# Order of a step's input loads, and the place of one gate tile, in a fused gated-linear-attention and FFN kernel

## The chip, the cores and the metric

The kernel runs on one core of a Trainium2 chip. The metric is device time of one execution in microseconds. A core has TensorE (PE in the profile, with its weight loads as PEld), VectorE (DVE), ScalarE (ACT), GpSimd (POOL), and SyncE (SP), which here issues nearly all DMAs from one queue in program order. Each engine runs its own instructions in order and waits on semaphores for the others.

## The reference

A recurrent attention over 32 heads-and-batches (batch 4, 8 heads, 768 positions, head size 48), and a feed-forward on its output with two multiplied gates and two further matrices:

```python
for t in range(S):
    state = alpha[:, :, t, :, None] * state + einsum('bhd,bhe->bhde', k[:, :, t], v[:, :, t])
    y[:, :, t] = einsum('bhd,bhde->bhe', q[:, :, t], state)
x = y.transpose(0, 2, 1, 3).reshape(B * S, H * D)        # 3072 x 384
out = ((x @ w1) * (x @ w2)) @ w3 @ w_out                 # d_ff 1024, out 3072 x 384
```

q, k, v and alpha come as float32, the four weights as float64.

## The kernel before, in words

**Tiling.** The sequence is cut into chunks of 128 positions, 6 to a batch, so N = 24 chunks over all. The loop of line 510 takes one chunk per step, n = 0 to 24. Three chunks make a group of 384 tokens, g = 0 to 7, on which the feed-forward gates work: one gate tile is `gate(g, f)`, 128 of the 1024 hidden columns for the 384 tokens of a group.

**Attention.** Within a chunk the decay is turned into sums of logarithms: `logs` (L246, ACT; from chunk 10 on also the casts L250 and L251) takes the logarithm of alpha, `decays` (L261 or L264) sums it on TensorE and takes two exponentials (L267, L268), and `decayed` (L277, DVE) multiplies k and q by them. `transposed` (L299, copied out at L301) turns k and q, `scores` (L339, masked at L342 on DVE) forms the products inside the chunk, `outer` (L311, added at L319 or L321) adds the chunk to the state, `attend_state` (L358) and `attend` (L364) form the output from the state and from the masked scores, and L368 copies it out. Every second chunk GpSimd rescales the state (`advance`, L328 to L330) by factors that go through DRAM (L253, L270, L272, L285). In one step these work on different chunks: `attend` on n - 1, `scores` and `outer` on n, `transposed` on n + 1, `decayed` on n + 2, `decays` on n + 3, `logs` on n + 4.

**Loads.** At the head of a step SP issues, in this order: the stores of x (L236) that the step before left, v of chunk n + 3 (L136, one of 5 buffers), alpha of chunk n + 5 (L124, 3 buffers), k and then q of chunk n + 4 (L130 and L131, 3 buffers). Later in the step come the weight loads (L181), the store of a finished gate tile (L419) and, in steps 4, 8, 12, 16 and 20, the load of a group's x back from DRAM (`load_x`, L379). A load waits until its buffer has been read; SP holds everything behind it meanwhile.

**Weights.** The float64 weights are taken apart as integers and put together as float32 on ACT and DVE (L189 to L199), a few instructions per step (`convert`). w1 and w2 are split into three parts each (L207, L209, L210), so that float32 products can be formed by fast matmuls.

**Gates.** Two steps after its load, in steps 6, 10, 14, 18 and 22, the x of a group is split in three (`split_x`: L385 on ACT, then L386 and L387 on DVE, each 128 by 1152). Half a gate tile is one call of `exact`: 6 matmuls of L396 into one PSUM bank, with the first and second part of the split, a scaled copy by ACT (L398), 3 matmuls of L400 into another bank, with the third part, and the sum on DVE (L401). Two halves are multiplied (L412) and stored (L419). The halves wait in a list, `fill`; `run(k)` puts k of them into the program at that point. From step 6 the number per step goes 0, 3, 3, 2, and starts again with every split: three places of a step take at most one half each.

```python
        pieces = (0, 3, 3, 2)[(n - 6) % 4] if n > 5 else 0
        ...
        run(pieces > 0)
        ...
        run(pieces > 1)
        ...
        run(pieces > 2)
```

Groups 0 to 3 put four of their eight tiles into the loop, group 4 (split in step 22, the last split of the loop) all eight into the list; steps 23 and 24 take three of these (six halves). Of the 64 tiles 45 are left for the time after the loop. There they run one after the other (line 572), with the conversion of w3 and w_out between them and, from some point on, a `fold` after a gate: w3 times w_out (L439, L441, L445 to L450), eight in all. When the last fold is done, buffers for the last stage are opened and the first four loads of stored gate tiles begin (L456). The last stage, `project`, splits these (L463 to L465) and multiplies them with the folded matrix (again L396 to L401), 24 times.

**Order of instructions.** The program text sets the order on PE and SP. On ACT and DVE the framework's scheduler orders the instructions by its own estimate of when their inputs come, so that a moved load can change their order too.

Of the kernel before, what the change touches and what calls it, by code (L numbers as in the profile page):

```python
# [48 lines left out]
def kernel(  # L49
# [27 lines left out]
    AHEAD = 4  # L77
# [39 lines left out]
    def rows(src, n):  # L117
        b, c = divmod(n, NCH)
        return src[b, :, ds(c * C, C), :].rearrange("h p d -> p h d")

    def load_a(n):
        if n < N:
            st["a", n] = inp.tile([C, H, D], FP32, tag="ac", name="ac")
            nc.sync.dma_start(out=st["a", n], in_=rows(alpha, n))  # L124

    def load_kq(n):
        if n >= N:
            return
        st["kq", n] = inp.tile([C, 2, H, D], FP32, tag="kq", name="kq")
        nc.sync.dma_start(out=st["kq", n][:, 0], in_=rows(k, n))  # L130
        nc.sync.dma_start(out=st["kq", n][:, 1], in_=rows(q, n))  # L131

    def load_v(n):
        if n < N:
            st["v", n] = vs[n % len(vs)]
            nc.sync.dma_start(out=st["v", n][:, :, 0:D], in_=rows(v, n))  # L136
# [77 lines left out]
    def convert(steps, ahead=3):  # L214

        for _ in range(steps):
            while weights and len(begun) < ahead:
                begun.append(weights.popleft())
                next(begun[-1])
            if not begun:  # L220
                return
            x = begun.popleft()
            try:
                next(x)
                begun.appendleft(x)
            except StopIteration:
                pass
# [4 lines left out]
    def store():  # L232

        while later:
            dst, src = later.popleft()
            nc.sync.dma_start(out=dst, in_=src)  # L236
# [4 lines left out]
    def logs(n):  # L241
        if n >= N:
            return
        a = st.pop(("a", n)).rearrange("p h d -> p (h d)")
        la = st["la", n] = work.tile([C, DM], FP32, tag="la", name="la")
        nc.scalar.activation(la, a, AF.Ln)  # L246
        if n >= LATE:

            t = st["la", n] = work.tile([C, 2, DM], FP32R, tag="la2", name="la2", bufs=1)
            nc.scalar.copy(t[:, 0], la)  # L250
            nc.vector.tensor_sub(t[:, 1], la, t[:, 0].bitcast(FP32))  # L251
        if n in ends:
            nc.gpsimd.dma_start(out=ends[n][2:3], in_=a[0:1])  # L253

    def decays(n):
        if n >= N:
            return
        lc = bank()[:, 0:DM]
        la = st.pop(("la", n))
        if n < LATE:  # L260
            nc.tensor.matmul(lc, utri if n % 2 else after, la, start=True, stop=True)  # L261
        else:
            for i in range(2):
                nc.tensor.matmul(lc, sums[:, n % 2], la[:, i], start=(i == 0), stop=(i == 1))  # L264

        e = st["e", n] = work.tile([C, 2, DM], FP32, tag="e", name="e", bufs=3)
        nc.scalar.activation(e[:, 0], lc, AF.Exp, scale=-1.0)  # L267
        nc.scalar.activation(e[:, 1], lc, AF.Exp)  # L268
        if n in ends:
            nc.gpsimd.dma_start(out=ends[n][0:1], in_=e[0:1, 0])  # L270
        if n + 1 in ends:
            nc.gpsimd.dma_start(out=ends[n + 1][1:2], in_=e[C - 1:C, 1])  # L272
        load_ends(n)
# [14 lines left out]
    def transposed(n):  # L288
        if n >= N:
            return  # L290
        qk = qks[n % 3]
        qkT = work.tile([C, 2, NP, C], FP32, tag="qkT", name="qkT")

        tp = [bank().rearrange("p (i j c) -> p i j c", i=2, j=NP) for _ in range(2)]
        for i in range(2):
            for j in range(NP):
                for half in range(2):
                    s = ds(DP * half, DP)
                    nc.tensor.transpose(tp[half][:, i, j, :], qk[s, i, 2 * j:2 * j + 2, :], ident[s, s])  # L299
        for half in range(2):  # L300
            nc.scalar.copy(qkT[:, :, :, ds(DP * half, DP)], tp[half])  # L301
        st["qkT", n] = qkT
# [20 lines left out]
    def advance(n):  # L323

        if n not in ends:
            return
        dec, d = work.tile([C, NP], FP32, tag="dec", name="dec"), decs[n // 2 % 2]
        nc.gpsimd.tensor_mul(dec, d[:, 0, :], d[:, 1, :])  # L328
        nc.gpsimd.tensor_mul(dec, dec, d[:, 2, :])
        nc.gpsimd.tensor_tensor(Ts[0][:, :, 0:D], st.pop(("T", n - 1)),  # L330
                                dec[:, :, None].to_broadcast([C, NP, D]), op=ALU.mult)

    def scores(n):
        qkT = st["qkT", n]
        sc = [bank().rearrange("p (j c) -> p j c", j=NP) for _ in range(2)]
        for j in range(NP):
            for i in range(2):
                r = ds(DP * i, D)
                nc.tensor.matmul(sc[i][:, j, :], qkT[r, 0, j, :], qkT[r, 1, j, :], start=True, stop=True)  # L339
        ms = work.tile([C, 2, NP, C], FP32, tag="ms", name="ms")  # L340
        for i in range(2):
            nc.vector.tensor_tensor(ms[:, i].bitcast(I32), sc[i].bitcast(I32), keep_bc, op=ALU.bitwise_and)  # L342
        st["ms", n] = ms
# [3 lines left out]
    def attend_state(n):  # L347
        qkT = st.pop(("qkT", n))

        y = [bank()[:, 0:HP * C].rearrange("p (j c) -> p j c", c=C) for _ in range(2)]
        st["y", n] = y, [(half * HP + j, i, y[i][ds(DP * half, DP), j, :])
                         for j in range(HP) for i in range(2) for half in range(2)]
        if n % NCH:
            for j, i, to in st["y", n][1]:
                r = ds(DP * i, D)
                nc.tensor.matmul(to, Ts[n % 2][r, j, :], qkT[r, 1, j, :],  # L358
                                 start=(j % HP == 0), stop=False, skip_group_check=True)
# [21 lines left out]
    def split_x(g, i):  # L381
        x = st.pop(("xT", g))
        t = tr[i].tile([C, 3, KM, TG], FP32R, tag="x3", name="x3")
        st["x3", g] = t
        nc.scalar.activation(t[:, 0], x, AF.Copy, scale=1.0 - 2.0 ** -13)  # L385
        nc.vector.tensor_sub(t[:, 1], x, t[:, 0].bitcast(FP32))  # L386
        nc.vector.scalar_tensor_tensor(t[:, 2], t[:, 0].bitcast(FP32), 1.0 + 1.0 / P, x,  # L387
                                       op0=ALU.mult, op1=ALU.subtract)
# [14 lines left out]
    def gate(g, f):  # L403
        r = []
        x = [[st["x3", g][:, part, kk, :] for kk in range(KM)] for part in range(3)]
        for i, scale in enumerate((1.0, P * P)):
            r.append(gw.tile([C, TG], FP32, tag="r", name="r"))
            exact(r[-1], [[w12[:, part, i, kk, ds(f * C, C)] for kk in range(KM)] for part in range(3)], x, scale)
            if len(r) == 1:
                yield  # L410
        ab = abp.tile([C, TG], FP32, tag="ab", name="ab")
        nc.vector.tensor_mul(ab, *r)  # L412
        store_ab()
        st["ab"] = g, f, ab
# [62 lines left out]
    def run(pieces):  # L477

        for _ in range(pieces):
            if not fill:  # L480
                return
            try:
                next(fill[0])
            except StopIteration:
                fill.popleft()
# [22 lines left out]
    begin = {4 + 4 * g: (g, range(FH if g < 4 else KF)) for g in range(5)}  # L508

    for n in range(N + 1):  # L510
        store()
        load_v(n + AHEAD - 1)
        load_a(n + 5)
        load_kq(n + AHEAD)
        if n:
            attend_state(n - 1)
        if n < N:
            scores(n)
        transposed(n + 1)
        if n - 2 in begin:  # L520
            g, tiles = begin[n - 2]
            split_x(g, 0)
            fill.extend(gate(g, f) for f in tiles)
        pieces = (0, 3, 3, 2)[(n - 6) % 4] if n > 5 else 0
        if n == 0:
            logs(2)
            decays(2)
            logs(3)
        early = n < 7
        convert(1, 2 if n == 0 else 3)  # L530
        advance(n)
        if n:
            attend(n - 1)
        outer(n)
        run(pieces > 0)
        if early:
            convert(1)
        decayed(n + 2)
        logs(n + 4)
        if n in begin:  # L540
            load_x(begin[n][0])
        convert(early and n > 2)
        run(pieces > 1)
        decays(n + 3)
        convert(early or n % 3 == 0)
        run(pieces > 2)
    store()
    part1.close()

# [79 lines left out]
```

## Time and profile before

| | us |
|---|---|
| median of 5 runs | 493.78 (491.25 to 495.92) |
| the profiled execution | 497.9 |
| its span, first to last instruction | 496.1 |
| mean granted TensorE clock in it | 0.976 of full |
| loop over chunks, to the last L364 | about 199 |
| PE of one gate tile at full clock (two times 1.04 and 0.52) | 3.12 |
| one projection on PE (2.77 and 1.39) | 4.16 |

The profile gives busy times per engine and, for the chain that ended last, what each piece waited for. A line of the chain has the start, the length and the work. A line of the timeline has the start, the length, the engine, the line of the kernel, the operation with its tiles and the count of instructions; in square brackets, where it applies, stands how long the engine was idle before it and what ended that idle time. The TensorE clock is either full (1.00) or half (0.50).

### The profile page before, as it was taken

How to read it: one execution, taken by the hardware profiler on the slowest of the kernel's cores; microseconds unless marked ns; L12 is line 12 of the kernel's file. 1: busy time of each engine (PE TensorE's matmuls, PEld its weight loads, DVE VectorE, ACT ScalarE, POOL GpSimd, SP SyncE). 2: the span in 40 equal slices, each digit the busy share in tenths (PEclk: the TensorE clock that was granted, in tenths of full speed). 3: DMA queues.
4: the chain of work that ended last, by engine and by line, in shares of the span. 5: the costliest groups of instructions: out<-in, count | busy, mean ns of one | idle time of the engine just before them, and what ended most of it. 6: DMA issues, size and time to landing. Idle time of an engine off the chain costs nothing.

```text
span 496.1 us, 9909 instructions
## 1 busy us (share of the span) xinstructions
PE 466.1 (94%) x3760; PEld 427.2 (86%) x3760; DVE 371.3 (75%) x620; ACT 250.1 (50%) x479; POOL 36.4 (7%) x83
## 2 busy tenths in 40 slices
PE   3788699999999998999999999999999999999997
PEld 1566489898998987999999988888888999999996
DVE  2779889997889575999999769686434787777771
ACT  2667667775667553555565345454223433333330
POOL 2132122121102200000000000000000000000000
PEclk9989989999799998999999999999999999999999
DMA  9999999899989963566555433320001886555511
GB/s 166 190 208 185 213 214 190 208 212 234 188 192 216 208 210 110 147 181 206 172 180 171 155 116 114 120 92 32 33 32 50 221 232 182 176 174 176 176 48 48
DMA packets 160496, 79.10 MB, mean 159 GB/s; under 512 B 104641, under 2 KB 154305, under 8 KB 160449
## 3 DMA queue, kind: packets, MB, share of 16 engines
q1 hardware_dynamic: 159168, 78.40, 62.4%
q0 software_dynamic: 1280, 0.08, 0.4%
q8 instruction: 29, 0.48, 0.4%
q14 instruction: 19, 0.15, 0.1%
HBM read 56.40 MB, written 22.06 MB: 158 GB/s over the span
## 4 chain that ended last, share of the span: by engine, by line
PE 84%; DMA 7%; ACT 3%; SPq 2%; DVE 2%; issue 1%; POOL 0%; ACTq 0%; POOLq 0%; DVEq 0%
PE bank L396 41%; PE bank L400 20%; PE bank L445 8%; PE bank L364 4%; PE bank L339 4%; DMA raw<-in_moe_w_dram 2%; PE bank L299 2%; PE bank L358 2%; PE bank L439 1%; DMA xd<-x 1%; DMA ac<-in_alpha_dram 1%; PE bank L311 1%; DMA dec<-ends 1%; PE bank L264 1%; DMA ends<-e 1%
## 5 line engine op out<-in xcount | busy, mean ns | idle before, releaser
L396 PE MATMUL bank<-x,w 128*128 128x384 f32 x768 | 161.4, 345 | 0.0
L396 PEld LDWEIGHTS bank<-x,w 128*128 128x128 f32 x768 | 136.4, 191 | 3.6 <-issue 0.5
L398 ACT ACTIVATE t<-bank 128x384 f32<-128x384 f32 x152 | 74.3, 491 | 116.7 <-PE bank L396 104.0
L401 DVE SCALAR_TENSOR_TENSOR r<-bank,t 128x384 f32<-128x384 f32 x128 | 69.7, 555 | 35.5 <-ACT t L398 29.4
L400 PE MATMUL bank<-x,w 128*128 128x384 f32 x384 | 87.5, 335 | 0.0
L396 PE MATMUL bank<-w3o,ab 128*128 128x384 f32 x384 | 70.4, 334 | 0.0
L400 PEld LDWEIGHTS bank<-x,w 128*128 128x128 f32 x384 | 69.0, 189 | 0.0
L396 PEld LDWEIGHTS bank<-w3o,ab 128*128 128x128 f32 x384 | 66.9, 188 | 0.0
L445 PE MATMUL bank<-wo,w3T 128*128 128x384 f32 x128 | 42.6, 486 | 0.0
L189 ACT ACTIVATE rest<-raw 128x512 f32<-128x512 uint32 (+1 forms) x36 | 23.4, 650 | 33.1 <-DMA raw<-in_moe_w_dram 25.8
L412 DVE TENSOR_TENSOR ab<-r 128x384 f32<-128x384 f32 x64 | 35.6, 557 | 2.2 <-DMA abd<-ab 1.4
L400 PE MATMUL bank<-w3o,ab 128*128 128x384 f32 x192 | 37.1, 334 | 0.0
L445 PEld LDWEIGHTS bank<-wo,w3T 128*128 128x128 f32 x128 | 24.2, 189 | 14.9
L464 DVE TENSOR_TENSOR ab<-abl,ab 128x1024 fp32r<-128x1024 f32 x24 | 29.4, 1225 | 9.1 <-ACT ab L463 9.1
L463 ACT ACTIVATE ab<-abl 128x1024 fp32r<-128x1024 f32 x24 | 25.5, 1062 | 19.0 <-PE bank L400 18.8
L339 PEld LDWEIGHTS bank<-qkT 48*128 48x128 f32 x384 | 25.0, 199 | 11.5 <-ACT qkT L301 5.6
L339 PE MATMUL bank<-qkT 48*128 48x128 f32 x384 | 29.8, 298 | 5.2 <-ACT qkT L301 3.0
L400 PEld LDWEIGHTS bank<-w3o,ab 128*128 128x128 f32 x192 | 33.6, 188 | 0.0
L342 DVE TENSOR_TENSOR ms<-bank,keep 128x512 int32<-128x512 int32 x48 | 31.2, 685 | 1.8 <-PE bank L339 1.8
L194 ACT ACTIVATE power<-power,rebias 128x512 uint32<-128x512 uint32 (+1 forms) x36 | 25.2, 702 | 11.5 <-DVE power L193 11.3
L277 DVE TENSOR_TENSOR qk<-kq,e 128x768 f32<-128x768 f32 x24 | 22.9, 954 | 9.7 <-ACT e L268 7.5
L401 DVE SCALAR_TENSOR_TENSOR o<-bank,t 128x384 f32<-128x384 f32 x24 | 13.4, 558 | 22.4 <-issue 13.7
(69 smaller groups left out, 544.7 us busy)
## 6 DMA issues: line engine op xcount, KB each, us to landing
abd<-ab SPq DMA_DIRECT2D x64, 192.0 KB, 2.6
abl<-abd SPq DMA_DIRECT2D x24, 512.0 KB, 4.5
raw<-in_moe_w_dram SPq DMA_DIRECT2D x16, 512.0 KB, 3.9
xT<-xd SPq DMA_DIRECT2D x12, 576.0 KB, 4.2
raw<-in_moe_w_dram SPq DMA_DIRECT2D x24, 256.0 KB, 4.9
ac<-in_alpha_dram SPq DMA_DIRECT2D x24, 192.0 KB, 5.0
kq<-in_k_dram SPq DMA_DIRECT2D x24, 192.0 KB, 5.2
kq<-in_q_dram SPq DMA_DIRECT2D x24, 192.0 KB, 4.3
```

The source lines that it names most:

```text
L189: nc.scalar.activation(rest, low, AF.Copy, scale=2.0 ** -52)
L194: nc.scalar.activation(power, power, AF.Relu, scale=2.0 ** 23, bias=rebias)
L339: nc.tensor.matmul(sc[i][:, j, :], qkT[r, 0, j, :], qkT[r, 1, j, :], start=True, stop=True)
L342: nc.vector.tensor_tensor(ms[:, i].bitcast(I32), sc[i].bitcast(I32), keep_bc, op=ALU.bitwise_and)
L396: nc.tensor.matmul(p1, w[part][i], x[part][i], start=(part == i == 0), stop=(part == 1 and i == n - 1))
L398: nc.scalar.activation(t, p1, AF.Copy, scale=(1.0 + 1.0 / P) * scale)
L400: nc.tensor.matmul(p2, w[2][i], x[2][i], start=(i == 0), stop=(i == n - 1))
L401: nc.vector.scalar_tensor_tensor(to, p2, -scale, t, op0=ALU.mult, op1=ALU.add)
L412: nc.vector.tensor_mul(ab, *r)
L445: nc.tensor.matmul(po, w3T[:, j, :], wo[:, j, :], start=(j == 0), stop=(j == KF - 1))
L463: nc.scalar.activation(t[:, 0], ab, AF.Copy, scale=1.0 - 2.0 ** -13)
L464: nc.vector.tensor_sub(t[:, 1], ab, t[:, 0].bitcast(FP32))
```

## The change

The four loads at the head of a step are issued with alpha first, then k and q, and v last. In the step of the last split, step 22, which takes no halves of gates today, the third place takes two: one whole gate tile of group 4. So one tile fewer is left after the loop, 44 instead of 45.

```diff
     for n in range(N + 1):
         store()
-        load_v(n + AHEAD - 1)
         load_a(n + 5)
         load_kq(n + AHEAD)
+        load_v(n + AHEAD - 1)
         if n:
             attend_state(n - 1)
...
         pieces = (0, 3, 3, 2)[(n - 6) % 4] if n > 5 else 0
+        final = n - 2 == max(begin)
...
         convert(early or n % 3 == 0)
-        run(pieces > 2)
+        run(2 if final else pieces > 2)
     store()
```

`begin` is the table of steps in which a group's x is loaded, so `max(begin)` is 20. In the list after the loop, the split of a further group is put in when four tiles are left before that group's first; with 44 tiles this falls on the first tile, with 45 on the second.

## The prediction

> **What bounds the kernel now.** I read the page's totals first, then the chain of work that ended last, then the timelines where that chain leaves TensorE.
>
> ```profile
> PE 466.1 (94%) x3760; PEld 427.2 (86%) x3760; DVE 371.3 (75%) x620; ACT 250.1 (50%) x479; POOL 36.4 (7%) x83
> ...
> PE 84%; DMA 7%; ACT 3%; SPq 2%; DVE 2%; issue 1%; POOL 0%; ACTq 0%; POOLq 0%; DVEq 0%
> ```
>
> The chain is 84% PE. In order of time it is PE without a break from 188.55 us to the end; the breaks that cost anything lie before. So a change pays only if PE stands less, or at less than full clock for less time, before 189 us. Up to about 64 us there are no gates, and the busy table in 5 us stretches shows DVE at 3.8 to 5.0 of 5 between 30 and 65: there the weight conversion on DVE sets the pace. From 70 to 121 PE is busy throughout but for 0.2 us near 92.
>
> **Part one: alpha, k, q, v instead of v, alpha, k, q.** No instruction is added; per step one v issue moves behind three others on SP. A v issue takes 0.41 us (at 50.15) to 1.05 us (at 18.46), so alpha, k and q leave that much earlier. v leaves later by three issues: around 50 us 0.90 + 2.51 + 2.17 = 5.6 us. It is for the outer product three steps later, and a step takes 7 to 9 us here; with that cover gone L311 would wait, and PE with it. The k issue waits for DVE (13 waits of L130, 22.2 us in all), and v used to slip in before that wait. Behind it now stand v and then the step's weight loads, ab store, xT load and the next x stores, each later by up to one v issue. I price that at 0 (bounds 0 and 1.05 us where one of them is late already), since the weight loads wait for DVE anyway (37.6 us at L181 in its three largest waits).
>
> Where is alpha late? Once on the chain:
>
> ```profile
> 50.60 6.87 DMA ac<-in_alpha_dram
> ...
> 57.50 0.52 ACT la L246
> 58.02 0.53 ACT w L207
> ...
> 58.58 0.42 DVE w L209
> ```
>
> ACT stood 0.53 us for it, so 0.53 is the most that this place can give. But L207 needs DVE's L199, which ended at 57.82, and it began at 57.93: with alpha in time it begins 0.1 us earlier. I take 0.1. q is late at 26.87 (DVE stood 1.68 us), but DVE's next work waits for weights that land at 29.56 and are not moved: 0.
>
> The compiled order also changes on ACT and DVE; on PE it does not until step 22. Three moves matter. (1) Near 32 us a 0.42 us L190 goes ahead of the L321 that waits 1.22 us for POOL: 0.3 gained. (2) Near 52 us the decayed qk (L277) goes ahead of L209, which could start at 51.72, and waits for an exponential I place at about 52.05 (L267 and L268 after a PE result near 50.6): 0.35 lost. (3) At the first gates:
>
> ```profile
> 66.88 0.49 ACT L398 ACTIVATE t<-bank 128x384 f32<-128x384 f32 x1 [2.64 <-PE bank L396]
> 67.27 0.64 ACT L368 COPY x<-bank 128x256 f32<-128x256 f32 x2
> 67.78 0.74 ACT L194 ACTIVATE power<-power,rebias 128x512 uint32<-128x512 uint32 x1
> 68.44 0.49 ACT L398 ACTIVATE t<-bank 128x384 f32<-128x384 f32 x1
> 68.83 0.52 ACT L246 ACTIVATE la<-ac 128x384 f32<-128x384 f32 x1
> 69.38 0.51 ACT L250 CAST la<-la 128x384 fp32r<-128x384 f32 x1
> ```
>
> PE stands 1.01 us until 69.94 for that last cast. In the new order the x copies come before the first L398, inside its 2.64 us of waiting, and the second L398 comes after the cast: 66.88 + 0.49 + 0.52 + 0.74 + 0.51, less overlaps of 0.1 each, ends near 69.0. That is 0.9 gained, and PE is full afterwards, so it is kept. Sum of part one: 0.1 + 0.3 - 0.35 + 0.9 = 0.95, taken as 0.9 us gained; bounds 1.4 gained (alpha worth 0.53) and, if DVE eats all of it and one late x store is 1.05 later, 1.4 lost.
>
> **Part two: one gate goes from after the loop into step 22.** It has 18 matmuls (two halves of 6 of L396, 1.04 us, and 3 of L400, 0.52 us), two L398 (0.49), two L401 (0.56), an L412 (0.56) and one ab store on SP (0.33 us to issue). Nothing is added in all; PE meets it right after the last outer product of the step, ahead of L358 and L339, which stand there now:
>
> ```profile
> 184.26 0.62 PE L311 MATMUL bank<-v,qk 128*64 128x48 f32 x16
> ...
> 184.69 1.35 DVE L386 TENSOR_TENSOR x<-xT,x 128x1152 fp32r<-128x1152 f32 x1
> ...
> 186.70 0.65 PE L358 MATMUL bank<-qkT,T 48*64 48x128 f32 x12 [1.46 <-DVE ms L342]
> ...
> 187.16 1.35 DVE L387 SCALAR_TENSOR_TENSOR x<-x,xT 128x1152 fp32r<-128x1152 f32 x1
> ...
> 188.55 1.17 PE L339 MATMUL bank<-qkT 48*128 48x128 f32 x16 [1.20 <-DVE x L387]
> ```
>
> It looks as if 2.66 us of standing could be filled with 3.12 us of gate. It can't, because the gate needs the split that DVE is making. The first third of a half (3 matmuls, 0.52 us) needs only ACT's part, there at 183.94: PE runs it at 184.86. The second third needs L386, ending 186.04: PE stands 0.7 us, runs 0.52. The last third needs L387, which stays behind two masks (L342) and ends 188.51: PE stands 1.9 us again. By 188.5 PE has done 6 of 18 matmuls, 1.04 us, and not the 0.60 us of L358: gained 0.4 us, not 3.1. Everything PE meets behind it (L358, L339, L364) finds its inputs ready, the copies of qkT and x being due by 189.05. The masks of step 23 now queue behind L401 and L412 on DVE and come near 193, for an L364 due near 197: hidden. The ab store waits on SP for L412, near 192; the x store behind it is not due before that. Bounds: 2.7 gained if DVE comes to L387 early, 0.5 lost if a bank is late.
>
> Then the clock. In stretches of 3.41 us (columns: stretch, length, PE busy, granted clock, DMA share, GB/s):
>
> ```profile
> 182.75:186.16 3.41, 2.49 (x51) 1.00 0.77 247
> 186.16:189.57 3.41, 1.67 (x28) 1.00 0.11 39
> 189.57:192.99 3.42, 3.42 (x24) 0.50 0.71 193
> ```
>
> After two stretches without a gate matmul the clock is halved for 3.4 us: L364 took 1.90 instead of 1.02 and L396 1.89 instead of 1.24, 1.5 us lost. The same stood before 124.7, at a price of 6.8 us at half clock, 3.4 us lost. Only 152.0 to 158.9 had no gate and kept its clock. The changed step puts 6 gate matmuls before 186.6 and more at 188.5, so both stretches hold some. I take the whole 1.5 us; the bounds are 0 (it falls anyway) and 3.4 gained (where it would have stayed 6.8 us).
>
> [...]
>
> Last, one gate fewer stands behind the last fold. The first ab loads are issued at 382.81 and the first projection begins at 392.40; without one gate (3.12 us) 6.5 us are left for the landing and a 1.06 us split:
>
> ```profile
> DMA to landing us min/median/max: 4.2/4.5/6.8
> ```
>
> 4.5 + 1.06 = 5.6 fits with 0.9 to spare; at 6.8 PE stands 1.4 us. I take 0, keep 1.4 lost.
>
> **Sum.** 0.9 + 0.4 + 1.5 + 0 = 2.8 us. The profiled execution took 497.9 us (span 496.1 and 1.8 around it) and becomes 495.1; it was 4.1 us above the median of the five runs, 493.78, part of which must be half-clock time that other executions have less of. Taken from the median: 491.0.
>
> **Rivals.** A measurement can tell about 0.5% (2.5 us) from no change.
> B, the clock falls anyway, or does not fall there in an ordinary run: 0.9 + 0.4 = 1.3, 492.5. For it: that two stretches without gates at 152 kept the clock shows that it is not sure to fall. Against it: the table above.
> C, slower: the shifted order makes another split step (step 18, PE busy only 2.41 of 3.41 us at 155.4; or step 10 at 90.6, 3.19) stand across two stretches, and the clock is halved for 6.8 us more, 3.4 lost; it decides if PE stands about 1 us more there, which a late x store or xT load behind v can do. With only the 0.4 kept: +3.0, 496.8. Against it: xT is needed two steps after its load.
> D, the order change also removes the standing at 121.7 to 125.3 (0.84 and 0.43 us) with its 3.4 us at half clock, since the exponential there no longer waits behind the x copies: 1.3 + 3.4 + 1.5 = 6.2, 487.6. Against it: the x copy still waits for its store to land (6.91 us).
> That the change does nothing it says is not so: the new orders of SP and PE are as described. That the filled standing only shifts is already in the 0.4.
>
> **How the numbers follow.** Forecast 0.40, B 0.27, C 0.18, D 0.15. The forecast lies just past the bound, so 0.28 of its 0.40 counts as faster, 0.12 as same. Faster: 0.28 + 0.15 = 0.43; same: 0.12 + 0.27 = 0.39; slower: 0.18. The range reaches to C and D, 487.5 to 497.0; the unknown bounds lie in it. The likeliest case alone, with the bounds of its small terms: 489.5 to 492.5.
>
> **What would show it.** Right: L400 of the new gate waits for L387 and PE still stands about 2.6 us around it; the granted clock stays at 1.00 after it; the cast before L264 ends a microsecond earlier after the first gates; no PE wait before the first projection. Wrong: a clock of 0.50 after step 22, a new half-clock stretch near 92 or 157, L311 waiting for v, or ACT's split waiting for ab loads.

## The result, and the profile after

The changed kernel takes 498.27 us (median of 22 runs, 494.69 to 500.15), the kernel before 494.80 (41 runs, 491.25 to 498.55). The ratio is 1.0064, with a 95% interval of 1.0044 to 1.0084: by the ratio it is 3.2 us slower (3.5 by the two medians), where 2.8 us faster was forecast. The profiled execution took 498.62 us (span 496.8, mean granted clock 0.978).

The two lines of totals, page of the changed kernel:

```profile
PE 470.0 (95%) x3760; PEld 428.5 (86%) x3760; DVE 373.3 (75%) x620; ACT 249.5 (50%) x479; POOL 37.3 (7%) x83
...
PE 61%; DVE 0%; ACT 0%; issue 0%; DVEq 0%
```

The kernel is bound as before. The same 3760 matmuls take 470.0 us where they took 466.1, at a mean clock of 0.978 where the first profile of the kernel before had 0.976, so these totals don't tell how much of the loss is clock. The chain can be followed back only to 186 us, the rest has to be read from timelines.

**A pair to compare.** Where half clock falls differs from execution to execution, and the first profile of the kernel before had 6.8 us of it from 124.7, where neither a second one (e12) nor the changed kernel has any. The second (span 491.4) has its first three half-clock stretches at 41.4, 55.1 and 65.3 us, the changed kernel's at 41.3, 55.0 and 65.2, e11's (below) at 41.5, 55.1 and 65.4. These three can be laid side by side. Rows are bounded by the first L364 of a step (chunk number) or of a stage; the gate that was moved (3.12 us) is taken out of step 22 and put back at the end.

| stretch, us | before (e12) | after | difference | e11 - e12 |
|---|---|---|---|---|
| start to chunk 6 | 65.27 | 64.61 | -0.66 | -0.53 |
| chunk 6 to 8, first gates | 20.81 | 22.61 | +1.80 | +0.50 |
| 8 to 13 | 36.31 | 36.57 | +0.26 | +0.09 |
| 13 to 14 | 4.21 | 5.16 | +0.95 | 0.00 |
| 14 to 21 | 54.51 | 54.43 | -0.08 | -0.26 |
| 21 to 23, step 22, less 3.12 | 11.93 | 13.70 | +1.77 | +0.66 |
| to the last fold | 183.28 | 183.28 | 0.00 | 0.00 |
| last fold to first projection, plus 3.12 | 11.41 | 12.58 | +1.17 | +1.16 |
| projections | 99.67 | 99.85 | +0.18 | +0.19 |
| sum | | | +5.39 | +1.81 |

The sums are the differences of the spans (5.4 and 1.8). By the ratio the loss is 3.2, so this pair shows some 2 us too much. A part of its differences is clock: from chunk 6 to 8 the changed kernel has 6.8 us at half clock, e12 and e11 3.4 each, and in step 22 it has 3.4 and they have none. At a loss of at most half (an estimate from the granted 0.50; the 16 matmuls of L364 took 1.90 us at half clock in before and 1.02 at full), that is up to 1.7 us of the +1.80 and of the +1.77. The largest differences lie at three places: the first gates, step 22, and the end of the gates. Chunk 13 to 14 comes back under Open.

**The first gates.** Timeline of the changed kernel:

```profile
64.61 1.44 PE L364 MATMUL bank<-ms,v 128*64 128x128 f32 x16
64.74 1.07 ACT L301 COPY qkT<-bank 128x512 f32<-128x512 f32 x2 [2.35 <-PE bank L299]
65.70 1.18 ACT L385 ACTIVATE x<-xT 128x1152 fp32r<-128x1152 f32 x1
...
66.92 0.36 DVE L321 TENSOR_TENSOR tmp<-bank,T 128x192 f32<-128x192 f32 x1 [1.90 <-PE bank L311]
...
66.93 1.33 PE L396 MATMUL bank<-x,w 128*128 128x384 f32 x3
67.20 1.35 DVE L386 TENSOR_TENSOR x<-xT,x 128x1152 fp32r<-128x1152 f32 x1
...
68.46 1.35 DVE L387 SCALAR_TENSOR_TENSOR x<-x,xT 128x1152 fp32r<-128x1152 f32 x1
```

and of the kernel before (e12), where chunk 6 comes 0.66 us later:

```profile
63.03 1.17 ACT L385 ACTIVATE x<-xT 128x1152 fp32r<-128x1152 f32 x1
...
65.27 1.94 PE L364 MATMUL bank<-ms,v 128*64 128x128 f32 x16
65.42 1.07 ACT L301 COPY qkT<-bank 128x512 f32<-128x512 f32 x2 [1.22 <-PE bank L299]
65.68 1.35 DVE L386 TENSOR_TENSOR x<-xT,x 128x1152 fp32r<-128x1152 f32 x1
...
66.95 1.35 DVE L387 SCALAR_TENSOR_TENSOR x<-x,xT 128x1152 fp32r<-128x1152 f32 x1
...
69.50 0.35 DVE L321 TENSOR_TENSOR tmp<-bank,T 128x192 f32<-128x192 f32 x1
```

Before, ACT makes its part of the first split (L385) at 63.03, while it has nothing else, and DVE its two at 65.68 and 66.95. After, L385 stands behind the two copies of step 7 (L301), which wait 2.35 us for TensorE; L386 and L387 stand behind the state update of step 7 (L321), which waits 1.90 us for TensorE. ACT is idle for these 2.35 us, and the split comes at 65.70, 67.20 and 68.46. TensorE runs the first gate half in pieces of three as the thirds arrive: it begins the first half 1.04 us earlier than in e12 (66.93, 67.97) and the second half 1.04 us later (71.06, 70.02). No load is waited for: in e7, with the same loads, L385 runs at 62.38.

The cast that the prediction spoke of, ACT in the changed kernel:

```profile
69.96 0.49 ACT L398 ACTIVATE t<-bank 128x384 f32<-128x384 f32 x1 [1.99 <-PE bank L396]
70.35 0.52 ACT L246 ACTIVATE la<-ac 128x384 f32<-128x384 f32 x1
71.19 0.72 ACT L194 ACTIVATE power<-power,rebias 128x512 uint32<-128x512 uint32 x1 [0.32 <-DVE power L193]
71.82 0.50 ACT L250 CAST la<-la 128x384 fp32r<-128x384 f32 x1
72.75 0.49 ACT L398 ACTIVATE t<-bank 128x384 f32<-128x384 f32 x1 [0.44 <-PE bank L396]
```

As forecast the x copies (L368) are gone from between and the second L398 comes last; the cast ends at 72.32, and TensorE gets to its L264 at 73.09 without a wait. ACT's wait of 0.53 us for alpha is gone too, but e12 doesn't have it either.

**Step 22.** TensorE in the changed kernel, and three stretches of 3.41 us (columns as in the prediction, with PEld, DVE, ACT and POOL busy after PE):

```profile
188.28 1.30 PE L400 MATMUL bank<-x,w 128*128 128x384 f32 x3 [1.76 <-DVE x L387]
```

```profile
181.27:184.68 3.41, 3.41 (x79) 3.17 (x80) 3.41 (x9) 2.92 (x5) 0.00 (x0) 1.00 0.54 156
184.68:188.09 3.41, 1.77 (x16) 1.07 (x12) 3.41 (x5) 1.72 (x5) 0.00 (x0) 1.00 0.36 138
188.09:191.51 3.42, 3.23 (x10) 3.27 (x11) 0.86 (x3) 0.85 (x3) 0.00 (x0) 0.50 0.38 86
```

The gate waits for its split as predicted (1.76 us for L387; 1.9 was forecast), and the clock falls all the same, for 3.41 us.

**The end.** TensorE and ACT of the changed kernel at the first projection:

```profile
391.26 0.69 PE L400 MATMUL bank<-x,w 128*128 128x384 f32 x3
392.95 1.89 PE L396 MATMUL bank<-w3o,ab 128*128 128x384 f32 x9 [1.00 <-ACT ab L463]
```

```profile
391.46 0.49 ACT L398 ACTIVATE t<-bank 128x384 f32<-128x384 f32 x1 [1.07 <-PE bank L396]
391.85 1.05 ACT L463 ACTIVATE ab<-abl 128x1024 fp32r<-128x1024 f32 x1
393.45 1.07 ACT L463 ACTIVATE ab<-abl 128x1024 fp32r<-128x1024 f32 x1 [0.55 <-DMA abl<-abd]
```

With one gate behind the last fold, ACT's split of the first stored tile (L463) begins at 391.85, right behind the L398 of the last gate, though its load had landed at 389.9, and the projection waits for it; the second split waits 0.55 us for its load.

### The profile page after: what moved, and what is told of

It is laid out like the page before. It is cut to its first block, busy times and chain, and to the rows that moved or that the text cites. A ratio compares the mean times of both kernels' runs of the same rounds, so it can differ in the third digit from the quotient of the medians.

```text
span 496.8 us, 9915 instructions
## 1 busy us (share of the span) xinstructions
PE 470.0 (95%) x3760; PEld 428.5 (86%) x3760; DVE 373.3 (75%) x620; ACT 249.5 (50%) x479; POOL 37.3 (7%) x83
## 4 chain that ended last, share of the span: by engine, by line
PE 61%; DVE 0%; ACT 0%; issue 0%; DVEq 0%
PE bank L396 34%; PE bank L400 17%; PE bank L445 8%; PE bank L439 1%; PE bank L364 0%; DVE x L387 0%; PE bank L358 0%; PE bank L339 0%; ACT ab L463 0%; DVE ms L342 0%; DVE o L401 0%; ACT t L398 0%; DVEq L401 0%
## 5 line engine op out<-in xcount | busy, mean ns | idle before, releaser
L398 ACT ACTIVATE t<-bank 128x384 f32<-128x384 f32 x152 | 74.3, 491 | 118.9 <-PE bank L396 104.2
L401 DVE SCALAR_TENSOR_TENSOR r<-bank,t 128x384 f32<-128x384 f32 x128 | 69.6, 555 | 36.9 <-ACT t L398 32.9
L339 PEld LDWEIGHTS bank<-qkT 48*128 48x128 f32 x384 | 26.0, 202 | 11.3 <-ACT qkT L301 4.1
L463 ACT ACTIVATE ab<-abl 128x1024 fp32r<-128x1024 f32 x24 | 25.5, 1063 | 20.1 <-PE bank L400 18.8
L339 PE MATMUL bank<-qkT 48*128 48x128 f32 x384 | 31.2, 302 | 4.2 <-ACT qkT L301 2.8
L301 ACT COPY qkT<-bank 128x512 f32<-128x512 f32 x48 | 25.9, 588 | 16.9 <-PE bank L299 16.9
L401 DVE SCALAR_TENSOR_TENSOR o<-bank,t 128x384 f32<-128x384 f32 x24 | 13.4, 557 | 22.6 <-issue 13.7
```

Of the source, the lines that this page charges most:

```text
L398: nc.scalar.activation(t, p1, AF.Copy, scale=(1.0 + 1.0 / P) * scale)
L401: nc.vector.scalar_tensor_tensor(to, p2, -scale, t, op0=ALU.mult, op1=ALU.add)
L463: nc.scalar.activation(t[:, 0], ab, AF.Copy, scale=1.0 - 2.0 ** -13)
```

## The experiments

The us column is (ratio - 1) times the median of the kernel before on the same chip (492.86 for e1 to e4, 494.42 for e5 to e8, 493.65 for e9 to e11). "Split's order" is the order on ACT and DVE at the first split: first, as before, or behind, as after.

| kernel | loads | split's order | gate in step 22 | fold earlier | ratio, 95% | us |
|---|---|---|---|---|---|---|
| after | new | behind | yes | no | 1.0064, 1.0044 to 1.0084 | +3.2 |
| e1 | new | behind | no | no | 1.0084, 1.0057 to 1.0112 | +4.1 |
| e2 | old | first | yes | no | 0.9990, 0.9966 to 1.0014 | -0.5 |
| e3 | new | behind | yes | yes | 1.0049, 1.0019 to 1.0080 | +2.4 |
| e4 | old | first | yes | yes | 0.9956, 0.9926 to 0.9986 | -2.2 |
| e5 | new in step 4 | behind | no | no | 1.0030, 1.0006 to 1.0054 | +1.5 |
| e6 | new but in step 4 | first | no | no | 0.9965, 0.9945 to 0.9986 | -1.7 |
| e7 | new | first, by hand | no | no | 0.9938, 0.9912 to 0.9964 | -3.1 |
| e8 | new | first, by hand | yes | yes | 0.9960, 0.9939 to 0.9981 | -2.0 |
| e9 | old | first | no | no | 0.9983, 0.9960 to 1.0005 | -0.8 |
| e10 | new, v after xT | first | no | no | 0.9929, 0.9903 to 0.9955 | -3.5 |
| e11 | new | first, by hand | yes | no | 1.0003, 0.9983 to 1.0023 | +0.1 |

**e1, the loads alone.**

```diff
-        load_v(n + AHEAD - 1)
         load_a(n + 5)
         load_kq(n + AHEAD)
+        load_v(n + AHEAD - 1)
```

> Only the order of the loads is changed (alpha, k, q, v), the gate tile stays after the loop. Theory 1 (the loss is in two places: about 1.4 us before the first projection, from the moved gate, and the rest, about 1.8 us, before the first gates, from the new order of loads and of ACT and DVE): 1.5 to 2.2 us slower than before. Theory 2 (all of the 3.2 us comes from the moved gate): within 0.8 us of before. Theory 3 (all of it comes from the loads; the moved gate pays back what it costs): 3 us slower.

It loses more than the whole change; Theory 3 comes nearest. TensorE's waits from chunk 6 to 8 (total, times, longest):

```profile
PE bank L400 <- DVE x L387: 0.9, 1, 0.9
PE bank L396 <- ACT x L385: 0.8, 1, 0.8
PE bank L396 <- DVE x L386: 0.6, 1, 0.6
PE bank L299 <- DVE r L401: 0.5, 1, 0.5
```

2.3 us for the three parts of the first split, and then half clock from 67.5 to 70.9: 23.09 us from chunk 6 to 8.

**e2, the gate alone.**

```diff
-        run(pieces > 2)
+        run(2 if n - 2 == max(begin) else pieces > 2)
```

> Only the gate tile is moved into step 22; the loads stay as before. Theory 1: 1.0 to 1.6 us slower, with PE standing 1.0 us for the first projection's split (L396 waiting for L463) and 2 us for L387 inside the moved gate. Theory 2: 3 us slower. Theory 3: within 0.5 us of before.

No difference that can be measured, as Theory 3 had it. The loss is in the loads.

**e3 and e4, an earlier fold**, with the whole change and with the gate alone: the count that spreads the conversions over the gates after the loop starts at 1.2, so the last fold has two gates behind it again.

```diff
-    owed = 0.0
+    owed = 1.2
```

> The whole change, and the weight conversion of the time after the loop is given one gate's share ahead (owed begins at 1.2), so that the last fold falls one gate earlier and two gates stand behind it again, as before the change. Theory 1: no wait before the first projection, and 1.4 us off the change: 1.5 to 2.0 us slower than before. Theory 2: if the moved gate costs by its tail alone, equal to before; if elsewhere, 3 us slower. Theory 3: 1.5 to 3 us slower.

> The gate tile is moved, the loads stay as before, and the last fold falls one gate earlier (owed begins at 1.2), so that two gates stand behind it. All theories have the tail's 1.4 us back against the gate moved alone. Theory 1: 0.4 us faster than before up to equal, and up to 2 us faster where the half clock after step 22 goes away. Theory 2: up to 1.5 us slower. Theory 3: 1.4 us faster.

In both profiles the time from the last fold to the first projection is 11.41 us with two gates, and TensorE does not wait there. e4 lies 1.7 us below e2 (e3 0.8 below after), about the 1.35 us that the table of stretches shows lost at the end; Theory 3 asked for 1.4 us faster in e4, and it is 2.2.

**e5 and e6, step 4.** In the compiled order the first split falls behind only if step 4 has the new order of loads, the step that issues the first xT. e5 has the new order in step 4 alone, e6 in all steps but this.

```diff
+        if n == 4:
+            load_a(n + 5)
+            load_kq(n + AHEAD)
+            load_v(n + AHEAD - 1)
+        else:
-        load_v(n + AHEAD - 1)
-        load_a(n + 5)
-        load_kq(n + AHEAD)
+            load_v(n + AHEAD - 1)
+            load_a(n + 5)
+            load_kq(n + AHEAD)
```

(e6: `if n != 4:`)

> The kernel before, with the new order of loads (alpha, k and q, v) in step 4 alone, the step that also issues the first load of xT. In the compiled order this one step already puts the scalar engine's split of the first xT (L385) behind a copy of the next keys and queries (L301), and VectorE's two split instructions (L386, L387) behind the next state update (L321). Theory A (the order of instructions at the first split costs the time): most of the loss of e1, +2.5 to +4.5 us against the kernel before, and attend 6 to attend 7 takes about 13.7 to 14.2 us instead of 10.8 to 12.5. Rival B (v and the x stores that land later in every step cost it): a 24th part of the loss, within 0.5 us of before. Rival C (no cause, the half-clock stretches fall at other places): also within 1 us.

> The complement: the new order of loads in every step but step 4. The compiled order of the first split is that of the kernel before. Theory A: the loss is gone, -1 to +0.8 us against before, attend 6 to 7 in 10.8 to 12.5 us. Rival B: nearly the whole loss stays, +3 to +4.5 us. Rival C: within 1 us of before, like e5.

e6 is faster than before, and by more than Theory A's range (-1 to +0.8; chunk 6 to 7 takes 9.65 us, below its 10.8 to 12.5 too), so late v and late x stores in all other steps cost nothing. e5 is slower, but by less than Theory A asked: no half clock came on top of its waits at the first gates in the profile. Waits of e5 at the first gates:

```profile
PE bank L400 <- DVE x L387: 0.9, 1, 0.9
PE bank L396 <- DVE x L386: 0.6, 1, 0.6
PE bank L264 <- ACT la L250: 0.5, 1, 0.5
PE bank L396 <- ACT x L385: 0.3, 1, 0.3
```

Chunk 6 to 8 takes 21.05 us at full clock, where five kernels with the split first (e2, e4, e6, e7, e8) take 19.75 to 19.97: 1.2 us. My expectation for chunk 6 to 7 (13.7 to 14.2) counted the half clock in and missed; it took 12.1.

**e7, the order alone.** e1 with step 7's copies (L301) queued behind the first split's ACT part, and its state update (L321) behind the split's last DVE part. Only the issue order on the two engines is named; `split` holds the first and last instruction of `split_x`.

```diff
-        transposed(n + 1)
+        with tc.issue_after(split[0].ins) if n == 7 else nullcontext():
+            transposed(n + 1)
...
-            split_x(g, 0)
+            split = split_x(g, 0)
...
-        outer(n)
+        with tc.issue_after(split[1].ins) if n == 7 else nullcontext():
+            outer(n)
```

> e1 (the new order of loads in all steps, the gate as before) with two issue orders named by hand: the keys' and queries' copies of step 7 (L301) are queued behind the first split's L385, and the state update of step 7 (L321) behind L387; no transfer is changed. Theory A: -1 to +0.8 us against the kernel before, attend 6 to 7 in 10.8 to 12.5 us. Rival B: the loss stays as in e1, +3 to +5 us, since v and xT land as late as there. Rival C: within 1 us of e1.

From +4.1 to -3.1 us by naming two issue orders, with every load where e1 has it. Waits at the first gates:

```profile
PE bank L400 <- DVE x L387: 0.3, 1, 0.3
PE bank L299 <- DVE r L401: 0.2, 1, 0.2
```

Rival B of this expectation (late v or xT) has fallen. The gain beyond before is larger than Theory A's range, and chunk 6 to 7 is shorter (9.67 us). But the two named orders moved more than the two instructions: by the traces, ACT and DVE run in another order than in e1 at some thirty places each, from step 7 to step 22, where e5 differs from before only between 61 and 84 us. So the 7.2 us are not all the first split's. Of the 6.8 us between the spans of the two profiles, 3.25 lie from chunk 6 to 8 (3.4 us of half clock in e1, none in e7), 0.94 from 13 to 14 and 4.50 in step 22 (6.8 us and none); e1 came to chunk 6 2.2 us earlier.

**e8**, the two orders of e7 in e3.

> The whole change with the two issue orders of e7 and the first conversion count raised by 1.2 as in e3, so that the last fold has two gates behind it again. Theory A: e7 and e4 added, so -3.2 to -1.2 us against the kernel before, the range of e4. Rival B: e3 again, +1.5 to +3.5 us.

4.4 us below e3, as Theory A says, but 1.1 us above e7: gate and fold, worth -2.2 with the old loads (e4), are worth nothing with the new ones.

**e9 and e12, the kernel before again.**

> The kernel before once more, under a name of its own, against itself: how far two sets of runs of one program lie apart, and where the half-clock stretches fall in a second profile of it. Both theories: a ratio between 0.998 and 1.002; in the profile the chain's places of half clock differ from those of the first profile, attend 6 to attend 8 takes 19.8 us where no half clock falls into it, against 21.4 us in the first profile with 4.9 us of half clock.

> The kernel before once more, for a second profile of it. Theory A: the waits that belong to its instruction order stand at the same places as in the first profile, wherever the half clock falls: at the first gate TensorE waits for the cast before L264 (1.0 us) and less than 0.5 us for the split; at step 22 it waits about 1.2 us before L339 and 1.0 to 1.5 us before L358. Attend 6 to 8 takes 19.8 us if no half clock falls into it. Rival C (the waits move with the half clock and belong to no order): the places and sizes differ by more than half.

Two sets of one program lie 0.8 us apart, the interval just holding 1. Differences under 1 us in the table say nothing. One execution of e9, the profiled one, took 1573 us at a granted clock of 1.00; the ratio leaves it out, its cause is open, and the second profile is e12's. In e12 the cast before L264 again cost 1.0 us and the split nothing. Step 22's waits kept their places, not their sizes: 1.4 us before L339 and 0.4 before L358, and L339's releaser was now the copy L301, whose output (qkT) it reads.

**e10, v still later**: alpha, k and q at the head of the step, v after the load of xT.

```diff
-        load_v(n + AHEAD - 1)
         load_a(n + 5)
         load_kq(n + AHEAD)
...
         if n in begin:
             load_x(begin[n][0])
+        load_v(n + AHEAD - 1)
```

> Alpha, k and q are issued first in every step, as in the changed kernel, and v is issued still later, after the load of xT of the same step, where before it was first. The compiled order of the first split is that of the kernel before without any order named by hand. Gate as before. Theory A (the order of instructions at the first split costs the time, and the earlier loads gain): -3.5 to -1 us against before, attend 6 to 8 in 19.7 to 20 us at full clock. Rival B (v that lands later costs it): +3 us or more, since v lands later here than in e1. Rival D (the two orders named by hand in e7 gain by themselves, the loads nothing): within 1 us of before.

The compiled order of the first split stays first without an order by hand. It has the lowest ratio of all, 0.9929, though not clear of e7's: v that leaves later than in the changed kernel costs nothing, and the gain of e7 doesn't come from naming an order (Rival D).

**e11, the two orders in the whole change.**

> The whole change with the two issue orders of e7 and nothing else, so without the earlier fold of e8. Theory A: the loads' -3.1 us of e7 and the gate's own price, the 1.4 us at the first projection less up to 1.4 us at step 22: -3.1 to -1.3 us against before, and after's loss of 3.2 us is gone by the two orders alone. Rival B: after again, +2 to +4 us.

after's loss is gone (1.0064 to 1.0003), but the gain of Theory A isn't there: the gate costs 3.2 us on top of e7. The table's last column shows where: 0.66 us in step 22 and 1.35 at the end against before, and against e7 (11.59 in step 22) 1.0 and 1.35. What is left between the profiles of e7 and e11, 1.5 us, lies from chunk 6 to 8, where e11 has 3.4 us of half clock and e7 none.

## Why the prediction was wrong

**The step that failed is the sum of part one**, "Three moves matter. (1) ... (2) ... (3)". It came to 0.9 us gained, and alone part one loses 4.1 (e1). There is a fourth in the same compiled order, at the same place: L385 behind L301, and L386 and L387 behind L321. I priced what the order change does to a cast at the first gates and not what it does to the split those gates need. Measured: 1.2 us of TensorE at full clock (e5), 2.3 us of waits in e1, and more half clock. From chunk 6 to 8 the four profiles with the split behind have 3.4 (e1), 6.8 (after), 3.4 (e3) and 0 us (e5) of it; with the split first five have none (e2, e4, e6 to e8), three 3.4 (e10 to e12) and the first of before 4.9. Named by hand, and with what else it moves, the order gives 7.2 us (e1 to e7), 4.4 (e3 to e8) and 3.0 (after to e11); e5, whose order leaves that of before only here, loses 1.5 (0.3 to 2.7). That it acts through order and not through transfers is shown by e7 and e10. How the rest divides between this place, the later places and the clock is not shown. How much of it is clock can be bounded from the granted clock of every run: 2 times (1 - clock) times the span is the time at half clock (in the profile of after 21.9 us, where its windows show six stretches of 3.41 us in the loop, 20.5, and 1.5 us at the end, 22.0 in all): on average 19.1 us in e1 and 14.1 in before on the same chip, 10.1 in e7 and 15.4 in before, 19.4 in after. At a loss of at most half, the 5.0 us more of e1 are up to 2.5 of its 4.1 us.

**The cast (0.9 gained, "PE is full afterwards, so it is kept").** The wait of 1.0 us before L264 stands in before, e2, e4 and e12 and is gone in after, e1, e3 and e6 to e8. It stands in e10 as well, the kernel with the lowest ratio (and with 0.5 and 0.4 us in e5 and e11). And where the split comes first the gain isn't kept. From chunk 6 to 7 e7 takes 9.67 us and e2 10.83; from 7 to 8 e7 takes 10.17 and e2 8.92. e7 meets there, in the middle of the next chunk's transposes:

```profile
74.39 0.43 PE L364 MATMUL bank<-ms,v 128*64 128x128 f32 x2
75.01 0.71 PE L299 MATMUL bank<-ident,qk 64*128 64x64 f32 x8 [0.19 <-DVE r L401]
75.65 0.98 PE L364 MATMUL bank<-ms,v 128*64 128x128 f32 x13
```

From its first L299 to the first L311 e2 takes 1.5 us (73.39 to 74.91), e7 2.6 (73.81 to 76.36), since the second eight transposes wait for a bank that L401 frees. In before PE was full afterwards, with 8.92 us from 7 to 8; e7, earlier by a microsecond, loses it there. In after, whose split is late in the same chunk, the cast's part can't be told apart.

**Alpha, L190 and L277 (sum 0.05).** after and e11 reach chunk 6 0.66 and 0.53 us before e12, but with 3.4 us less half clock on the way. That isn't told apart from 0.

**The price of late v, 0.** Right (e6, e7, e10).

**The gate (0.4 gained).** The working held: it waits 1.76 us for L387, as forecast. What it replaces was mis-sized. The prediction took 2.66 us of waits from one profile; the second has 1.8 and e7 1.4:

```profile
PE bank L358 <- DVE ms L342: 1.4, 1, 1.4
```

At full clock step 22 takes 11.93 (before), 11.59 (e7) and 11.18 us (e10) without the gate, and less 3.12 us 11.66 (e2) and 12.59 (e11) with it. The gate puts one wait in the place of another: with the old loads it gains 0.3 us, and against e7, where the wait before L339 is gone, it loses 1.0. The wait before L339 is gone in e6, e7 and e10; e1, with the loads of e7, still has it (1.4 us for L301), so the loads alone don't explain that.

**The clock (1.5 gained, "both stretches hold some").** Wrong, and the prediction's rival B was right here: in step 22 it fell in four of six profiles with the gate (after, e3, e4, e8, where the step takes 16.59 to 17.30 us; not e2 and e11, 14.78 and 15.71) and in four of seven without (before, e1, e5, e6, 13.08 to 16.08 us; not e7, e10, e12, 11.18 to 11.93). A gate matmul in each stretch was not what kept it: the stretch of after that held six was followed by half clock. Nor was a pair of stretches without one always followed by it: in the first profile of the kernel before six in a row have none (39.39 to 59.87 us), at a clock of 1.00. Within step 22 the profiles part by how much of one stretch TensorE is busy. In e11, with the same gate and the same 1.76 us of waiting, the wait lies across a border of two stretches:

```profile
181.43:184.85 3.42, 2.53 (x34) 1.84 (x28) 3.42 (x6) 2.22 (x6) 0.00 (x0) 1.00 0.64 190
184.85:188.26 3.41, 2.12 (x12) 2.06 (x12) 2.43 (x4) 1.46 (x5) 0.00 (x0) 1.00 0.55 132
```

and the clock stays at 1.00 (6 and 12 gate matmuls), where after had 1.77 of 3.41 in one.

**The end (0, bound 1.4 lost).** The bound was nearly the value: 1.17 us at the first projection and 0.18 behind. 5.6 us for landing and split left ACT out, on which L463 queues behind the last L398.

**The rivals.** C (slower, 496.8) comes nearest in kind and in size: a split step that stands and loses clock. Its place was another, the first split, and its cause "a late x store or xT load" was wrong. Its objection, "xT is needed two steps after its load", is true: xT was there, and the instruction that reads it was queued elsewhere. Of the distance between 491.0 and 498.27, 1.0 us is the kernel before itself, 494.80 in 41 runs where the prediction had 493.78 from five. D found nothing to remove: e12, the kernel before in a second profile, does not stand in these steps and has no half clock there, so the standing at 121.7 to 125.3 is not in every execution of it.

**Open.** Chunk 13 to 14 takes 5.15 us in after, e1 and e3, 4.21 in e2, e6, e7, e10 to e12, but also 5.14 in e4, and the trace shows only 0.2 us of waits there. And that e7 and e10 beat before by 3 us is argued, not shown: step 22 gives 0.3 to 0.75 us, and less half clock (10.1 and 11.2 us on average, where before has 15.4 and 16.9) up to 2.7 and 2.9.

## What to carry to other kernels

When a scheduler orders ACT and DVE, a moved load can change their order: list every instruction that changed places in front of the busiest engine's next need, and ask of each which other instruction now waits behind it. A wait that is filled with work that needs the same late input only changes its name. Fix the order you want by hand, or move the load to where the order stays, before judging a change of loads, and look what else that moves.

## What the runs showed of the clock

The half-clock stretches begin on a grid of 3.41 us whose phase differs from execution to execution. In after they begin at 41.32, 54.97, 65.21 and 188.09 us, the last three 4, 7 and 43 times 3.413 us behind the first; in before at 32.56, 59.87, 124.72 and 189.57, and there it is 8, 27 and 46 times. In both each lasts one or two stretches, at 0.50 throughout. In after the clock fell behind a stretch in which TensorE was busy 1.77 of 3.41 us, and the longest gap was 1.76 us; in before, in the same step, behind one with 1.67 us, at waits of 1.46 and 1.20 us.

In step 22 the busy time of a stretch parts the profiles: the clock fell after the eight stretches with 0.74 to 1.97 us and stayed after those with 2.12 and more (e2, e7, e11, e12); in e10, where it stayed too, TensorE's waits in the step come to 1.0 us. Over the whole loop busy time alone does not decide. In e12 the clock fell after 2.12 us (61.93 to 65.34), in before after 2.50 (121.31 to 124.72) and in after after 2.52 (37.91 to 41.32); it stayed after 1.89 in e5 (65.00 to 68.40) and after 1.74 in before (46.21 to 49.63). What else counts is open.

In step 22 after and e11 run the same matmuls in the same order and take, less 3.12 us, 13.70 and 12.59 us, with the same wait of 1.76 us, which in after falls almost whole into one stretch and in e11 is parted between two. One stretch at half clock costs at most 1.7 us, half of 3.41, by the estimate above, so one profile of each kernel is too few to price such a place.
